# One output unit per hidden tile and whole batch, with the activation computed by Softplus and Erf over four units

## The chip, the core and the metric

The kernel runs on one core of a Trainium2 chip. The metric is the device time of one launch in microseconds (us); lower is better. The core's engines are PE (TensorE: matrix products), DVE (VectorE) and ACT (ScalarE) for elementwise work, POOL (GpSimd) and SP (SyncE), which here mainly issue DMAs. PE multiplies a *stationary* operand, loaded by a weight-load instruction (PEld in the profile), with a *moving* operand that streams through column by column; results go to PSUM, eight banks of 512 fp32 columns, and ACT or DVE copy them out.

## What is computed

```python
def _attn_ref(q, k, v, p):                 # 8 batches, 8 heads, 576 positions, 64 wide; p has 32 packed queries
    p_packed = sm_attn(p, k, v)            # softmax(p k^T / 8) v
    return sm_attn(q, p_packed, p_packed)  # softmax(q p_packed^T / 8) p_packed

def _moe_ref(x, w_in, w_out):              # x: 4608 tokens x 512; w_in 512 x 2048; w_out 2048 x 512
    h = x @ w_in
    sp = np.maximum(h, 0.0) + np.log1p(np.exp(-np.abs(h)))
    g = h * erf(sp)
    return g @ w_out
```

The weights arrive as 64-bit floats and are converted to 32 bits on the chip; everything else is fp32.

## The kernel before

**Tiling.** A batch has 576 tokens, taken as two halves of 288 columns (`HT`). The 2048 hidden features are 16 tiles `f` of 128; a unit is (batch b, half c, pair i of f tiles), 128 units in all. Batches 0 and 1 are gone through in two turns (`TURNS`: first half of the features for both, then the second), so that the weights can arrive meanwhile; batches 2 to 7 each run through all features.

**Products.** Attention's last product is folded into the hidden layer: `w_prime` (L243) multiplies the packed values `pt[b]` with a block of 512 columns of w_in, so that h = a2 x w', with `a2[b]` the second softmax. Precise products are made from values split into a high and a low part of type fp32r (fp32, rounded so that one pass suffices): hi x hi, hi x lo and lo x hi, three matmuls summed in PSUM. In `h_block` (L264) the two f tiles of a unit take 6 matmuls of 288 columns each (two halves r of the contraction, three terms), with w' stationary. In `o_block` (L308) w_out is stationary and g moves: 4 output tiles d x 2 f tiles x 3 terms = 24 matmuls of 288 columns, so the output is built transposed (`outT`) in four PSUM banks, `ps_o0` to `ps_o3`. The first 12 units (`WHOLE`) use unsplit fp32 operands instead, one call per product, because w_out is split later (`split_w_out`, L103, L104).

**The activation** is composed of tables that share a set: ACT halves h on the way out of PSUM (L267, bank pair `ps_h`), then Tanh, Square, Tanh (L270 to L272), DVE two scalar_tensor_tensor (L273, L274), ACT a last Tanh (L275), DVE a product (L283) and the split into `gh` (L286) and `gl` (L287). All of these work on one unit, 576 columns.

**Attention** is a generator of twelve stages: first scores (L165), softmax, transposes (L186), packed values (L198), second scores (L212), transposes and softmax by DVE, split (L232, L233). It and `w_prime` share one PSUM tile of two banks, `ps_m`. It is emitted in stages between the units of the batch before.

**Weights.** `load_f32` loads 64-bit values through SP's queue and converts them by one ACT operation (L87) and three DVE operations (L88 to L90), 512 columns at a time.

**Order.** A plan places loads, attention stages and w' blocks at unit numbers; `o_block` follows `h_block` by `LAG` = 3 units. Within that, a planner orders the instructions of each engine by a simulated timeline (`schedule_with_timeline_sim=True`), the order of emission being the priority. All loads and the first store of a tile go through SP's queue; the second turn of batches 0 and 1 adds onto its output through POOL's queue (L318).

Of the kernel before, what the change touches and what calls it, by code (L numbers as in the profile page):

```python
# [8 lines left out]
F32 = mybir.dt.float32  # L9
# [8 lines left out]

T_SCALE, T_BIAS = 0.2627170245906788, -0.9287499984171923
Q_SCALE, Q_BIAS = 1.2484601345862187, 1.2510285994602417  # L20
U_SCALE, U_BIAS = 2.981034033350855, 0.5025259929887246
A1, A2 = -1.0780370417831138, 7.315330971479113
A_SCALE, A_BIAS = 0.5000167827005251, 0.3105391086974029

# [4 lines left out]
def tile_pack_attention_moe(ctx: ExitStack, tc: tile.TileContext, qT, kT, v, pT, w_in, w_out, outT):  # L29
    nc = tc.nc  # L30
# [5 lines left out]
    NDM = DM // P  # L36
    FB = 512
    NFB = DFF // FB
    NBLK = DFF // (2 * P)
# [5 lines left out]
    LAG = 3  # L45
    NB0 = 2
    TURNS = (0, NBLK // 2, NBLK)
    WHOLE = 12
    SPLIT = 14
    WI_AT = (-1, 1)  # L50
    ATT1 = (0, 2)
    ATT2 = 14
    CONV = 2

    EARLY = ("wpl", "wpl", "wph", "wph", "wpl", "wpl")
# [3 lines left out]
    opool = ctx.enter_context(tc.tile_pool(name="wo", bufs=2 * (DFF // P) + 1))  # L59
    spool = ctx.enter_context(tc.tile_pool(name="stage", bufs=2))  # L60
    wpool = ctx.enter_context(tc.tile_pool(name="wp", bufs=NFB))
    tpool = ctx.enter_context(tc.tile_pool(name="tmp", bufs=3))
# [3 lines left out]

    ident = cpool.tile([P, P], F32, name="ident")
    bias = cpool.tile([P, 4], F32, name="bias")
    w_in_sb = cpool.tile([P, 4, DFF], F32, name="w_in_sb")
    wo, wo_hi, wo_lo = {}, {}, {}  # L70
    nc.scalar.preload_act_table_set("exp_and_others")
    make_identity(nc, ident)
    for i, c in enumerate((T_BIAS, Q_BIAS, U_BIAS, A_BIAS)):
        nc.vector.memset(bias[:, i:i + 1], c)

    def load_f32(dst, src, name, pool=None, tag="wst"):
# [5 lines left out]
        st = (pool or spool).tile([P, n], I64, name=name, tag=tag)  # L82
        nc.sync.dma_start(st[:], src)
        words = st[:].bitcast(U32).rearrange("p (n two) -> p n two", two=2)
        low, high = words[:, :, 0], words[:, :, 1]
        bits = dst.bitcast(U32)
        nc.scalar.activation(dst, high.bitcast(F32), AF.Abs, scale=F64_SCALE)  # L87
# [4 lines left out]
    def load_w_in(j, c, **slot):  # L92
        load_f32(w_in_sb[:, c, j * FB:(j + 1) * FB], w_in[c * P:(c + 1) * P, j * FB:(j + 1) * FB], f"wi{j}_{c}", **slot)

    def load_w_out(f, **slot):
        made = opool.tile([P, DM], F32, name=f"wo{f}", tag="wo")
        load_f32(made[:], w_out[f * P:(f + 1) * P, :], f"wos{f}", **slot)
        wo[f] = made

    def split_w_out(f):  # L100
        hi = opool.tile([P, DM], F32R, name=f"woh{f}", tag="wo")
        lo = opool.tile([P, DM], F32R, name=f"wol{f}", tag="wo")
        nc.scalar.copy(hi[:], wo[f][:])  # L103
        nc.vector.tensor_tensor(lo[:], wo[f][:], hi[:], op=ALU.subtract)  # L104
        wo_hi[f], wo_lo[f] = hi, lo

    a2 = {}
    pt = {}
    wp = {}

    STAGES = 12
    PACKS = 8

    def attention(b, roomy=False):
# [5 lines left out]
        def chunk(name, tag="kvq"):  # L120
            if tag == "kvq":
                return apool.tile([P, S], F32, name=f"{name}_{b}", tag="kvq", bufs=6)[:]
            return tpool.tile([P, S], F32, name=f"{name}_{b}", tag=tag)[:]

        def bank(name):

            turn[0] += 1
            if roomy and turn[0] % 3:
                d = turn[0] % 3 * 2 - 2
                return [ps_o.tile([P, 512], F32, name=f"{name}_{b}_{x}", tag=f"ps_o{d + x}")[:] for x in range(2)], None  # L130
            ps = ps_m.tile([P, 2, 512], F32, name=f"{name}_{b}", tag="ps_m")
            return [ps[:, 0, :], ps[:, 1, :]], ps
# [10 lines left out]
        p = apool.tile([P, NC, NK], F32, name=f"p{b}", tag="p")  # L143
        nc.sync.dma_start(p[:], pT[b])
        k = [chunk(f"k{c}") for c in range(NC)]
        for c in range(NC):
            nc.sync.dma_start(k[c], kT[b, :, c, :])
        yield
        v_at = ("hs", "hs", "hs", "kvq", "kvq") if roomy else ("kvq",) * NCH
        values = [chunk(f"v{j}", v_at[j]) for j in range(NCH)]  # L150
        for j in range(NCH):
            n = min(P, S - j * P)
            nc.sync.dma_start(values[j][0:n, 0:2 * NC * 64], v[b, j * P:j * P + n, :])
        yield
        q_at = ("t0", "t0", "t0", "t1") if roomy else ("kvq",) * NC
        q = [chunk(f"q{c}", q_at[c]) for c in range(NC)]
        for c in range(NC):
            nc.sync.dma_start(q[c], qT[b, :, c, :])
        yield
# [28 lines left out]
        yield  # L188
        banks = bank("p")
# [4 lines left out]
        for j in range(NCH):  # L194
            n = min(P, S - j * P)
            for c in range(NC):
                for r in range(2):
                    nc.tensor.matmul(po[64 * r:64 * r + 64, NK * c:NK * c + NK],  # L198
                                     values[j][0:n, 64 * (2 * c + r):64 * (2 * c + r) + 64],
# [37 lines left out]
    def w_prime(b, j):  # L237
# [8 lines left out]
        nc.vector.tensor_tensor(lo[:], ps[:], hi[:], op=ALU.subtract)  # L246
        wp[b, j] = (hi, lo)

    gs = {}

    def h_block(b, c, i, whole):

# [41 lines left out]
    def o_block(b, c, i, first, last):  # L294
# [16 lines left out]
        if not last:  # L311
            return
# [160 lines left out]
```

## Time and profile before

| | |
|---|---|
| three runs | 790.92, 792.65 (median), 794.25 us |
| profiled execution | 789.89 us; its span from first to last instruction 788.1 us |
| mean granted TensorE clock | 0.968 |
| HBM read, written | 45.61 MB, 11.80 MB |
| matmuls and weight loads | 6256 each |

The profile shows one execution. Busy times of one engine can overlap with those of another, and matmuls of PE overlap with each other: the recorded duration of a matmul contains the way through the array, so the distance between two starts says what one costs in a stream. A group's row reads: line, engine, operation, output<-inputs, shapes, count | busy us, mean ns of one | idle time of the engine just before them, and what ended it. In the slices a digit is a tenth of the slice.

### The profile page before, as it was taken

The page shows a single profiled execution, that of the slowest core. Times are in us where ns is not written, and L with a number is a line of the kernel's source. Part 1 is how long each engine was busy: PE and PEld are TensorE (multiplying, and loading weights), DVE is VectorE, ACT ScalarE, POOL GpSimd, SP SyncE. Part 2 cuts the span into 40 slices and gives each one's busy share as a digit, 9 for nine tenths or more (in the row PEclk, how much of TensorE's full clock was granted, in tenths as well). Part 3 has the DMA queues.
Part 4 walks back from the last instruction along what each step waited for, and adds up shares of the span by engine and source line. Part 5 has one row for each costly group of instructions (what it writes and reads, how often), then busy time and mean ns, then how long its engine had stood idle before and what let it go on. Part 6 is the DMA issues. An engine that isn't in the chain of part 4 may idle for free.

```text
span 788.1 us, 15219 instructions
## 1 busy us (share of the span) xinstructions
PE 744.6 (94%) x6256; PEld 664.1 (84%) x6256; DVE 599.7 (76%) x916; ACT 597.6 (76%) x1011; POOL 15.1 (2%) x22
## 2 busy tenths in 40 slices
PE   3549988999999999999999999999999999999998
PEld 2228756899998898899799998889888998899998
DVE  3887898977689678867887769767886769766664
ACT  3357778988689878887687868778687867878784
POOL 0000000000111100000000000000000000000000
PEclk8568999999999999999999999999999999999999
DMA  8834735002542422013200222002300210000000
GB/s 306 291 110 149 243 116 162 31 17 67 107 88 31 83 76 89 1 39 98 80 32 1 83 81 72 13 1 80 132 32 1 79 47 1 31 2 31 1 31 31
DMA packets 31813, 58.39 MB, mean 74 GB/s; under 512 B 3584, under 2 KB 14848, under 8 KB 31744
## 3 DMA queue, kind: packets, MB, share of 16 engines
q1 hardware_dynamic: 29440, 55.06, 21.5%
q0 software_dynamic: 2304, 2.36, 2.6%
q8 instruction: 49, 0.80, 0.4%
q14 instruction: 20, 0.16, 0.1%
HBM read 45.61 MB, written 11.80 MB: 73 GB/s over the span
## 4 chain that ended last, share of the span: by engine, by line
PE 82%; DVE 7%; DMA 6%; ACT 3%; issue 1%; SPq 0%; ACTq 0%
PE o L308 50%; PE h L264 24%; PE wp L243 4%; DMA wi<-w_in 4%; DMA wos<-w_out 2%; PE p L198 2%; PE s L212 1%; PE s L165 1%; PE t L186 1%; DVE w_in_sb L89 1%; ACT t L270 1%; DVE wo L89 1%; ACT wo L87 1%; DVE w_in_sb L90 1%; DVE g L280 0%
## 5 line engine op out<-in xcount | busy, mean ns | idle before, releaser
L308 PE MATMUL o<-gl,woh 128*128 128x288 f32 x928 | 273.3, 295 | 0.0
L308 PE MATMUL o<-gh,woh 128*128 128x288 f32 x928 | 273.1, 300 | 0.0
L308 PE MATMUL o<-gh,wol 128*128 128x288 f32 x928 | 272.9, 295 | 0.0
L308 PEld LDWEIGHTS o<-gh,woh 128*128 128x128 f32 x928 | 172.1, 187 | 25.5 <-DVE t L273 8.9
L308 PEld LDWEIGHTS o<-gl,woh 128*128 128x128 f32 x928 | 174.3, 188 | 1.8 <-issue 1.3
L308 PEld LDWEIGHTS o<-gh,wol 128*128 128x128 f32 x928 | 174.6, 188 | 1.5 <-issue 1.3
L267 ACT ACTIVATE hs<-h 128x288 f32<-128x288 f32 x256 | 103.2, 412 | 95.4 <-PE h L264 94.6
L264 PE MATMUL h<-a2h,wph 128*128 128x288 f32 x512 | 155.2, 304 | 10.6 <-ACT wph L245 5.9
L264 PE MATMUL h<-a2l,wph 128*128 128x288 f32 x512 | 152.7, 298 | 1.8 <-DVE a2l L233 1.8
L264 PE MATMUL h<-a2h,wpl 128*128 128x288 f32 x512 | 152.6, 298 | 0.0
L283 DVE SCALAR_TENSOR_TENSOR hs<-t,hs 128x576 f32<-128x576 f32 x116 | 87.7, 756 | 72.5 <-ACT t L275 72.5
L275 ACT ACTIVATE t<-t,bias 128x576 f32<-128x576 f32 x128 | 98.8, 772 | 25.3 <-DVE t L274 25.0
L264 PEld LDWEIGHTS h<-a2h,wph 128*128 128x128 f32 x512 | 97.2, 190 | 22.3 <-ACT wph L245 6.8
L273 DVE SCALAR_TENSOR_TENSOR t<-t,hs 128x576 f32<-128x576 f32 x128 | 95.9, 750 | 20.1 <-ACT u L272 19.8
L270 ACT ACTIVATE t<-hs,bias 128x576 f32<-128x576 f32 x128 | 99.6, 778 | 2.9
L271 ACT ACTIVATE t<-t,bias 128x576 f32<-128x576 f32 x128 | 99.3, 775 | 2.3
L264 PEld LDWEIGHTS h<-a2l,wph 128*128 128x128 f32 x512 | 97.4, 190 | 4.3 <-DVE a2l L233 2.8
L272 ACT ACTIVATE u<-t,bias 128x576 f32<-128x576 f32 x128 | 99.3, 776 | 1.8
L264 PEld LDWEIGHTS h<-a2h,wpl 128*128 128x128 f32 x512 | 97.3, 190 | 1.9 <-issue 1.9
L274 DVE SCALAR_TENSOR_TENSOR t<-u,t 128x576 f32<-128x576 f32 x128 | 96.3, 752 | 1.6
L287 DVE TENSOR_TENSOR gl<-hs,gh 128x576 fp32r<-128x576 f32 x116 | 87.3, 753 | 1.5
L286 DVE CAST gh<-hs 128x576 fp32r<-128x576 f32 x116 | 52.9, 456 | 35.0 <-PE o L308 33.8
(60 smaller groups left out, 637.3 us busy)
## 6 DMA issues: line engine op xcount, KB each, us to landing
k<-kT SPq DMA_DIRECT2D x32, 288.0 KB, 4.3
q<-qT SPq DMA_DIRECT2D x32, 288.0 KB, 4.3
outT<-ob SPq DMA_DIRECT2D x64, 144.0 KB, 1.8
wi<-w_in SPq DMA_DIRECT2D x16, 512.0 KB, 6.0
v<-v SPq DMA_DIRECT2D x32, 256.0 KB, 3.6
wos<-w_out SPq DMA_DIRECT2D x16, 512.0 KB, 3.6
outT<-ob POOLq DMA_DIRECT2D x16, 144.0 KB, 3.7
v<-v SPq DMA_DIRECT2D x8, 128.0 KB, 4.2
```

The lines of the kernel that those rows point to most:

```text
L264: nc.tensor.matmul(ps[:, 0:HT], w[:, r, fo:fo + P], a[:, r, c * HT:(c + 1) * HT], start=(n == 0), stop=(n == 5))
L267: nc.scalar.mul(hs[:, k, :], ps[:, 0:HT], 0.5)
L270: nc.scalar.activation(t[:], hs[:], AF.Tanh, bias=bias[:, 0:1], scale=2.0 * T_SCALE)
L271: nc.scalar.activation(t[:], t[:], AF.Square, bias=bias[:, 1:2], scale=Q_SCALE)
L272: nc.scalar.activation(u[:], t[:], AF.Tanh, bias=bias[:, 2:3], scale=U_SCALE)
L273: nc.vector.scalar_tensor_tensor(t[:], t[:], 0.5 * A2, hs[:], op0=ALU.mult, op1=ALU.add)
L274: nc.vector.scalar_tensor_tensor(t[:], u[:], 0.5 * A1, t[:], op0=ALU.mult, op1=ALU.add)
L275: nc.scalar.activation(t[:], t[:], AF.Tanh, bias=bias[:, 3:4], scale=2.0 * A_SCALE)
L283: nc.vector.scalar_tensor_tensor(hs[:], t[:], 1.0, hs[:], op0=ALU.add, op1=ALU.mult)
L286: nc.vector.tensor_copy(ghi[:], hs[:])
L287: nc.vector.tensor_tensor(glo[:], hs[:], ghi[:], op=ALU.subtract)
L308: nc.tensor.matmul(acc[b, c][d][:, 0:HT], w[f][:, d * P:(d + 1) * P], gg[:, k, :], start=(first and k == 0 and n == 0), stop=(last and k = ...
```

## The change

One unit becomes (batch b, one f tile) over the whole 576 columns, still 128 units in the same two turns. What changes in it:

- **Output.** In `o_unit` g is stationary (128 tokens x 128 features) and w_out moves in 512 columns; the output is [token, column] and is no longer transposed. A batch has four full token tiles, one PSUM bank each; its last 64 tokens (`REM`) are copied by a DMA on SP's queue (`keep_rest`, one for each unit) into a tile `rest` beside the 64 of the partner batch, and `Rest` computes the shared 128 rows of two batches in one block of 48 matmuls, in the PSUM tile of attention and w'. Evictions alternate between ACT and DVE.
- **All units are split**: there are no fp32 output products any more, and `load_w_out` splits w_out as soon as it is loaded.
- **Activation.** h is copied out unscaled for four units into one tile of 2304 columns; Softplus and Erf run over it at once; DVE multiplies by h and splits, a unit at a time. The `t` tile has one buffer, `hs` two (of four units), `g` four (of one unit).
- **Lag.** `LAG` is 7 units. The plan has a group's Softplus at the head of the slot after its last h, and Erf and the products a slot later.
- **Weights.** The first 512 columns of w_in come in two halves (`load_w_in(0, 2, c)`, `load_w_in(2, 2, c)`), each with its own w' block, and batch 0's attention is emitted under `tc.high_priority()`.

The diff, cut to its core:

```diff
-    LAG = 3
-    WHOLE = 12
+    G = 4
+    LAG = 2 * G - 1
+    TURNS = (0, NF // 2, NF)
...
+    BUFS = {"hs": 2, "t": 1, "wo": 1, "g": 4, "ob": 2, "kvq": 5}
...
+    def load_w_in(f0, nf, c):
+        cols = slice(f0 * P, (f0 + nf) * P)
+        load_f32(w_in_sb[:, c, cols], w_in[c * P:(c + 1) * P, cols], f"wi{f0}_{c}")
+
+    def load_w_out(f):
...
+        load_f32(whole, w_out[f * P:(f + 1) * P, :], f"wos{f}")
+        nc.scalar.copy(hi[:], whole)
+        nc.vector.tensor_tensor(lo[:], whole, hi[:], op=ALU.subtract)
...
+    def keep_rest(b, f):
+        side = b % 2 * REM
...
+        nc.sync.dma_start(rest_of(f)[:, :, side:side + REM].bitcast(F32), gs[b, f][:, :, NT * P:S].bitcast(F32))
+
+    def h_unit(b, f):
...
+        for c in range(2):
+            ps = ps_h.tile([P, 512], F32, name=f"h{b}_{f}_{c}", tag="h")
...
+            nc.scalar.copy(hs[u // G][:, u % G, c * HT:(c + 1) * HT], ps[:, 0:HT])
-        nc.scalar.activation(t[:], hs[:], AF.Tanh, bias=bias[:, 0:1], scale=2.0 * T_SCALE)
-        nc.scalar.activation(t[:], t[:], AF.Square, bias=bias[:, 1:2], scale=Q_SCALE)
-        nc.scalar.activation(u[:], t[:], AF.Tanh, bias=bias[:, 2:3], scale=U_SCALE)
-        nc.vector.scalar_tensor_tensor(t[:], t[:], 0.5 * A2, hs[:], op0=ALU.mult, op1=ALU.add)
-        nc.vector.scalar_tensor_tensor(t[:], u[:], 0.5 * A1, t[:], op0=ALU.mult, op1=ALU.add)
-        nc.scalar.activation(t[:], t[:], AF.Tanh, bias=bias[:, 3:4], scale=2.0 * A_SCALE)
+    def softplus(k):
+        ts[k] = tmp([P, G, S], F32, f"t{k}", "t")
+        nc.scalar.activation(ts[k][:], hs[k][:], AF.Softplus)
+
+    def gate(k):
+        t, h = ts.pop(k), hs.pop(k)
+        nc.scalar.activation(t[:], t[:], AF.Erf)
+        for i in range(G):
+            b, f = units[k * G + i][:2]
+            nc.vector.tensor_tensor(h[:, i, :], t[:, i, :], h[:, i, :], op=ALU.mult)
+            g = tmp([P, 2, S], F32R, f"g{b}_{f}", "g")
+            nc.vector.tensor_copy(g[:, 0, :], h[:, i, :])
+            nc.vector.tensor_tensor(g[:, 1, :], h[:, i, :], g[:, 0, :], op=ALU.subtract)
+            gs[b, f] = g
+            if b % 2:
+                keep_rest(b, f)
...
+    def evict(po, where, add, on_act):
+        ob = tmp([P, DM], F32, f"ob{where[0][0]}_{len(where)}_{add}", "ob")
+        if on_act:
+            nc.scalar.copy(ob[:], po)
+        else:
+            nc.vector.tensor_copy(ob[:], po)
...
+    def terms(g):
+        return lambda f, cols: ((g[:, 0, cols], wo_hi[f]), (g[:, 1, cols], wo_hi[f]), (g[:, 0, cols], wo_lo[f]))
+
+    def o_unit(b, f, first, last):
+        if b % 2 == 0:
+            keep_rest(b, f)
+        g = gs.pop((b, f))
...
+        for t in range(NT):
+            po = acc[b][t][:]
+            for n, (x, w) in enumerate(terms(g)(f, slice(t * P, t * P + P))):
+                nc.tensor.matmul(po, x, w[:], start=(first and n == 0), stop=(last and n == 2))
+            if last:
+                evict(po, [(b * S + t * P, 0, P)], b in begun, t % 2 == 0)
...
+    class Rest:
+        def run(self, n):
+            for f in range(self.f, min(self.f + n, NF)):
+                for k, (x, w) in enumerate(terms(rest_of(f))(f, slice(0, P))):
+                    nc.tensor.matmul(self.po, x, w[:], start=(f == 0 and k == 0), stop=(f == NF - 1 and k == 2))
...
+        at(k * G + G, "f", ("sp", k))
+        at(k * G + G + 1, "f", ("gate", k))
...
+    def slot(n, o=()):
+        do(n, "f")
+        while late:
+            late.pop(0)()
+        do(n, "pre")
+        if n < N:
+            h_unit(*units[n][:2])
+        do(n, "post")
+        for k in o:
+            o_unit(*units[k])
...
+    for n in range(N + LAG):
+        slot(n, (n - LAG,) if n >= LAG else ())
+        if n < N:
+            b, f, _, last = units[n - LAG]
+            if n >= LAG and last and b % 2 and f == NF - 1:
+                Rest(b, ps_m.tile([P, 2, 512], F32, name=f"rest{b}", tag="m")[:, 0, :]).run(NF)
+            continue
+        tail = tail or Rest(B - 1, ps_m.tile([P, 2, 512], F32, name="rest_tail", tag="m")[:, 0, :])
+        tail.run(2 if n < N + LAG - 1 else NF)
```

The plan for the rest, in words: p and k of a batch are asked for twelve slots into the batch two before it, v and q three and eight slots into the batch before it; attention's nine stages lie between slots 0 and 14 of the batch before; a w' block comes two or three slots ahead of its first unit.

More of the change, by code (lines that the diff above doesn't have):

```diff
@@ L90, in load_f32 @@
         nc.vector.scalar_tensor_tensor(bits, low, 29, bits, op0=ALU.logical_shift_right, op1=ALU.bitwise_or)
[L92 to L104, printed above, removed]
-        wo_hi[f], wo_lo[f] = hi, lo
@@ L141, in copy_out @@
                 nc.scalar.copy(dst[:, x, :], parts[x][:, 0:n])
[L143 to L159, printed above, removed]
+        p, k = loaded.pop(("p", b)), loaded.pop(("k", b))
         a1 = apool.tile([P, 2, S], F32, name=f"a1_{b}", tag="big")
@@ new lines, in slot @@
+    def slot(n, o=()):
[8 more added lines that the diff above has]
+            o_unit(*units[k])
+    with tc.high_priority():
+        load("p", 0)
+        load("k", 0)
+        first = attention(0, roomy=True)
+        next(first)
+        next(first)
+    for c in range(NC):
+        load_w_in(0, 2, c)
+    with tc.high_priority():
+        load("v", 0, "hs")
+        load("q", 0, "t")
+        for _ in range(5):
+            next(first)
+        w_prime(0, 0, 2)
+        next(first)
+        next(first)
@@ L437 @@
+    while late:
+        late.pop(0)()
 def kernel(**inputs):
```

353 lines of the change are left out of this document (144 added, 209 removed).

## The prediction

> **What bounds the kernel now.** I read the page first: busy time by engine, the slices, the chain that ended last.
>
> ```profile
> span 788.1 us, 15219 instructions
> PE 744.6 (94%) x6256; PEld 664.1 (84%) x6256; DVE 599.7 (76%) x916; ACT 597.6 (76%) x1011; POOL 15.1 (2%) x22
> PE   3549988999999999999999999999999999999998
> PEclk8568999999999999999999999999999999999999
> PE 82%; DVE 7%; DMA 6%; ACT 3%; issue 1%; SPq 0%; ACTq 0%
> ```
>
> From the fifth slice or so (about 100 us) PE is full, and 82% of the chain is PE. The profiled execution took 789.89 us, 1.8 us around a span of 788.1; the median of the three runs shown is 792.65. So there are two stages: a start in which PE waits, and a long stage that costs what PE's instructions cost. The chain in order of time gives the long stage's period: the product that makes the packed values (L198) comes once a batch.
>
> ```profile
> 369.21 2.57 PE p L198 x80
> 640.30 2.57 PE p L198 x80
> ```
>
> These are three batches apart: (640.30 - 369.21) / 3 = 90.4 us a batch. The timeline of PE alone says what one instruction costs there: an output matmul, the hidden layer after it, and the fp32 output matmuls of the first units.
>
> ```profile
> 500.04 0.29 PE L308 MATMUL o<-gl,woh 128*128 128x288 f32 x1
> ...
> 502.17 0.29 PE L308 MATMUL o<-gh,wol 128*128 128x288 f32 x1
> 502.30 0.29 PE L264 MATMUL h<-a2h,wph 128*128 128x288 f32 x1
> ...
> 146.84 0.41 PE L308 MATMUL o<-g,wo 128*128 128x288 f32 x1
> 147.81 0.41 PE L308 MATMUL o<-g,wo 128*128 128x288 f32 x1
> ...
> 47.46 0.44 PE L264 MATMUL h<-a2h,wpl 128*128 128x288 f32 x1
> 47.70 0.44 PE L264 MATMUL h<-a2l,wph 128*128 128x288 f32 x1
> ```
>
> The durations overlap, so I go by starts. From 500.04 to 502.17 there are 16 steps: 133 ns for one 288-column matmul. A batch has 192 of L264 and 384 of L308, 576 x 0.1333 = 76.8 us. The other 13.6 us of 90.4 are attention and w'; PE has no idle time left.
>
> **The matmul's step, on which most hangs.** At half clock (47.46 to 47.70; 0.53 granted, windows below) the 288 columns take 240 ns, so at full clock the columns alone are 120, and 133 holds 13 more. The fp32 matmul is issued as two instructions a call (192 for 12 units of 8 calls), and four steps take 0.97 us (146.84 to 147.81; the three starts between are left out): 242 ns each, twice 120 and 2 more. So the 13 is no fixed charge on every matmul. It looks like a floor, the weight load that a 128x288 matmul at full clock is too short to cover. A 512-column matmul streams 120 x 512/288 = 213 and should cover it: I take 213.3 + 2.4 = 215.7 ns. Ends: 213.3, and 237 if time simply goes with columns (133.3 x 512/288); 13.3 as a fixed charge gives 226.7. The value nearest to the 242 ns row, which is nearest in length, is 215.7.
>
> The Trainium skill (TensorE: Matmul & The Clock Gate, section "Wait — 56ns, not 53.3ns?") states columns over 2.4 GHz plus 2.5 ns. It would give 122.5 for 288 columns, where this trace shows 133; the 242 ns row agrees with it. By that rule the new step is 215.8 and the old output loses nothing to loads, which the row refutes.
>
> **The sum on PE.**
>
> ```profile
> L308 PE MATMUL o<-gl,woh 128*128 128x288 f32 x928 | 273.3, 295 | 0.0
> L308 PE MATMUL o<-g,wo 128*128 128x288 f32 x192 | 51.5, 423 | 1.8 <-DVE g L280 1.8
> L243 PE MATMUL wp<-w_in_sb,pt 64*32 64x512 f32 x512 | 41.4, 615 | 8.1 <-DVE ta L215 3.9 <-DVE wpl L246 2.3 <-DVE w_in_sb L90 1.9
> ```
>
> Output before: 3 x 928 x 0.1333 + 192 x 0.2425 = 417.7 us. After: 128 units of 4 token tiles and 3 terms are 1536 matmuls, and the left-over 64 rows of two batches share a tile, 4 pairs x 16 f x 3 = 192; 1728 x 0.2157 = 372.7. Columns are equal if the fp32 ones are counted as three terms (3072 x 288 = 1728 x 512): the gain is purely the floor and the early fp32 units. Hidden layer: 1536 of 288 columns in both, unchanged; w' 33 blocks for 32; attention unchanged.
> In each of the last six batches: 384 x 0.1333 = 51.2 against (192 + 24) x 0.2157 = 46.6. **6 x 4.6 = 27.6 us less**, if PE stays the limit.
>
> **Does PE stay the limit?** The groups by line:
>
> ```profile
> L267 ACT ACTIVATE hs<-h 128x288 f32<-128x288 f32 x256 | 103.2, 412 | 95.4 <-PE h L264 94.6
> L270 ACT ACTIVATE t<-hs,bias 128x576 f32<-128x576 f32 x128 | 99.6, 778 | 2.9
> L222 ACT ACTIVATE ta<-ta 128x1152 f32<-128x1152 f32 x8 | 9.3, 1166 | 9.0 <-DVE ta L221 8.9
> L103 ACT CAST woh<-wo 128x512 fp32r<-128x512 f32 x16 | 10.1, 634 | 0.6 <-DVE wo L90 0.4
> L245 ACT CAST wph<-wp 128x1024 fp32r<-128x1024 f32 x32 | 31.9, 998 | 2.4 <-PE wp L243 2.4
> L138 ACT COPY a1t<-t 128x1024 f32<-128x1024 f32 x8 | 8.1, 1014 | 6.0 <-PE t L186 6.0
> L71 ACT ACT_TABLE_LOAD x1 | 1.3, 1283 | 0.7 <-PEq L465 0.7
> L273 DVE SCALAR_TENSOR_TENSOR t<-t,hs 128x576 f32<-128x576 f32 x128 | 95.9, 750 | 20.1 <-ACT u L272 19.8
> L286 DVE CAST gh<-hs 128x576 fp32r<-128x576 f32 x116 | 52.9, 456 | 35.0 <-PE o L308 33.8
> L287 DVE TENSOR_TENSOR gl<-hs,gh 128x576 fp32r<-128x576 f32 x116 | 87.3, 753 | 1.5
> ```
>
> ACT before, a unit: 2 x 0.41 + 4 x 0.78 = 3.9 us. After, four units: 8 x 0.41, and Softplus and Erf over 2304 columns. Their cost is not in the trace; from L103 to L222 ACT adds 0.532 us for 640 columns, 0.83 ns each, so 1.166 + 1152 x 0.00083 = 2.12 us each (below, nothing: the copies stay; above, four of 576 at 0.78, 3.1 us). Whether they share a table with Exp no row shows: one load serves Tanh, Square and Exp now. Ends: no load, and two loads a group and two more a batch, 10 x 1.28. I take the latter. A batch then has 32 x 0.41 + 8 x 2.12 + 10 x 1.28 = 43, and 12 for attention, w' and evictions: 55 of 86 us, against some 77 of 90 before (16 x 3.9 and 14). DVE: three scalar_tensor_tensor, a cast and a subtract (3.5 us a unit) become a multiply, a cast and a subtract, 1.96. Over the last six batches both lie beside PE and what they lose costs nothing.
> The new evictions of 512 columns (40 and 4, for 80 of 288) alternate ACT and DVE; hidden by the 9 matmuls of the other three banks, 1.9 us. The 128 copies of 64 columns into the left-over tile are new DMAs on SP's queue, each waiting for its g; behind them stand k, p, v, q loads, asked for some three slots (15 us) ahead. I cost them at nothing; uncovered, a batch's attention would start late by a landing of 2 to 4 us. A left-over block (48 matmuls, 10.4 us) holds the PSUM pair of attention and w' once in two batches; they have 16 slots, so I cost that at nothing too, and at its 10.4 us four times if attention became late. Because h and o now lie seven units apart, the final gate (two loads, two wide ACTs, DVE: 9 us) runs under three output units and their share of the left-over rows, 12 us. The end is again a copy and a store, about 3 us.
>
> **The start.** The windows, with the long second one from the first h to the end of batch 1, and the first h in the timeline:
>
> ```profile
> core 0: us, PE busy (x) PEld busy (x) DVE busy (x) ACT busy (x) POOL busy (x), PEclk, DMA share, GB/s
> 30.00:40.00 10.00, 3.18 (x32) 0.48 (x32) 8.67 (x13) 5.76 (x8) 0.00 (x0) 0.50 0.75 277
> 40.00:50.00 10.00, 5.65 (x35) 4.39 (x36) 10.00 (x17) 3.56 (x6) 0.00 (x0) 0.53 0.40 109
> 42.50:246.00 203.50, 188.20 (x1415) 157.08 (x1416) 168.59 (x265) 161.43 (x283) 10.49 (x12) 0.95 0.38 107
> ```
>
> ```profile
> 42.53 0.85 PE L264 MATMUL h<-a2h,wph 128*128 128x288 f32 x2 [4.24 <-ACT a2h L232]
> ```
>
> And DVE's share of the start, by line:
>
> ```profile
> L88 DVE TENSOR_SCALAR wo<-wo 128x512 uint32<-128x512 uint32 x16 | 6.7, 416 | 3.2 <-ACT wo L87 3.1
> L90 DVE SCALAR_TENSOR_TENSOR wo<-wos,wo 128x512 uint32<-128x512 uint32 x16 | 10.9, 684 | 0.0
> L104 DVE TENSOR_TENSOR wol<-wo,woh 128x512 fp32r<-128x512 f32 x16 | 11.0, 685 | 0.7 <-ACT woh L103 0.6
> L233 DVE TENSOR_TENSOR a2l<-tb,a2h 128x1152 fp32r<-128x1152 f32 x8 | 10.8, 1353 | 1.2 <-ACT a2h L232 1.2
> L246 DVE TENSOR_TENSOR wpl<-wp,wph 128x1024 fp32r<-128x1024 f32 x32 | 38.9, 1216 | 6.1 <-ACT wph L245 5.0
> ```
>
> Before the first h DVE is full with conversions. The change converts only two f columns (four half chunks) ahead of w' and gives attention the priority, so the first h comes at about 39 us (36 if DVE never delays attention, 42.5 if nothing is won).
> Before, batches 0 and 1 end at 785 (last matmul) - 6 x 90.4 + 9 (the last has no attention beside it) = 252. From 42.5 that is 209.5, of which PE needs 51.2 (h) + 46.6 + 64 (12 fp32 units, 20 of 3.2) + 27.2 (two attentions and w') = 189; 20.5 are stalls and cold clock.
> After, PE needs 51.2 + 432 x 0.2157 + 27.2 = 171.6. DVE needs 14 w_in chunks of 1.8 us (two shift-and-or of 0.68, a shift of 0.42), 16 w_out of 2.47, 32 gates of 1.96, two attentions of 13.5 (seven operations over 1152 columns at 1.35 and some 4 us of small ones), 8 w' of 1.22: 164. That is nearly PE's need, so the start cannot be as dense: DVE was 83% busy in that window (168.59 of 203.5), and 164 / 0.83 = 198. I take 198 us, from 39 to 237: **15 us less than 252**. Bounds: 184 (PE's need and 12 of stalls), 219 (DVE at 75%).
>
> **Sum:** 789.9 - 27.6 - 15 = 747 on the profiled execution's scale; the runs shown lie 2.8 above it: **750 us**, 5% less.
>
> **Rivals.**
> *Pitch.* The 13 ns belong to every fp32r matmul (226.7 ns), or go with columns (237): +19 to +37, 769 to 787. For it: no 512-column fp32r row exists. Against: the 242 ns row.
> *Start.* With 7 units between h and o, and gates of four, DVE and ACT (some 139 us: 64 copies 26, 16 wide ones 34, 20 loads 26, conversions 31, two attentions and w' 22) take turns at blocking PE: DVE at 75%, 219 us, 771. The other way, PE-limited, 184: 736, with an earlier first h 732.
> *ACT blocks the hidden layer: slower.* h has two PSUM banks, emptied by ACT in order. If a group's Softplus and Erf run back to back, ACT is away 2 x (1.28 + 2.12) = 6.8 us, and both halves of the next h are copied at 7.6; PE meanwhile has o and a slot's share of attention (12 x 0.2157 + 13.6 / 16 = 3.4), h (1.6), and o again: 8.4. The margin is 0.8 us. Each microsecond over it costs 32 us in all; from 2.2 us more a pair (42 us in all) the kernel is slower than before. An a1t copy and a w' cast (1.0 us each) caught between come near, in some groups. If a switch costs twice the load's 1.28 us (what goes ahead of a later load, no row shows), a pair has 2.56 more: 750 + 32 x 1.76 = 806. Against: the plan puts a slot between the two, and then each has its own cover.
> The Trainium skill (ScalarE: Activation LUTs, section "What ACT_TABLE_LOAD costs") speaks for this rival: every switch also drains, about 1380 ns, which the one load here, with nothing ahead of it, cannot show; by it the sum would be some 813.
> *It doesn't do what it says:* the planner scatters the wide activations and holds PE back as much as is saved: 790.
>
> **Chances.** Forecast 0.50 (own range 738 to 762); quicker start 0.10; slower start 0.15; pitch 0.10; no gain 0.03; ACT blocks 0.12. The range leaves out ACT's, no gain, and the top of pitch: 730 to 784. A measurement of this kernel tells about 0.5% from no change: faster 0.85, same 0.03, slower 0.12.
>
> **What would show it.** Steps of 216 ns between output matmuls right, 227 or 237 wrong; L198's counterpart every 86 us; first h near 39; table loads 80 in all; PE idle behind "hs" on ACT in mid-kernel would mean ACT blocks. Wrong if the period exceeds 88 us or batch 1 ends after 250.

## The result, and the profile after

The changed kernel takes **841.7 us** (median of four runs, 839.9 to 846.5) where the kernel before takes 791.8 on the same chip: a ratio of 1.064, with a 95% interval of 1.060 to 1.067. It was forecast 5% faster and is 6% slower; the time lies outside the range. The page of the changed kernel, with its span, busy times, the slices of PE, the chain, and the groups that the forecast had priced:

```profile
span 841.0 us, 12325 instructions
...
PE 754.3 (90%) x5024; PEld 589.4 (70%) x5024; DVE 439.9 (52%) x713; ACT 452.1 (54%) x589; POOL 7.9 (1%) x14
...
PE   3468687989999999989999999899999999899987
...
PE 56%; ACT 21%; DVE 14%; issue 4%; DMA 4%; SPq 0%; DVEq 0%; ACTq 0%
...
L278 DVE TENSOR_TENSOR hs<-t,hs 128x576 f32<-128x576 f32 x128 | 88.5, 754 | 222.3 <-ACT t L275 222.3
...
L270 ACT ACTIVATE t<-hs 128x2304 f32<-128x2304 f32 x32 | 68.1, 2130 | 0.4
...
L270 ACT ACT_TABLE_LOAD x32 | 41.1, 1283 | 0.6
L275 ACT ACT_TABLE_LOAD x32 | 41.1, 1283 | 0.6
```

ACT and DVE have *less* to do than before (452 us against 598, 440 against 600), as forecast, and their prices were right: 2.13 us for a wide operation (2.12 forecast), 0.75 for the multiply, 1.28 for a table load. Yet PE's share of the chain fell from 82% to 56%, and ACT's rose from 3% to 21%. No engine is full any more, which means that they wait for each other. The view of waits of PE's matmuls (who waited for what; us in total, times, longest) says where PE waits:

```profile
PE h L263 <- ACT hs L266: 20.3, 14, 3.2
PE o L314 <- DVE g L280: 13.3, 9, 5.8
...
PE o L314 <- DVE g L281: 3.5, 6, 1.9
```

The hidden layer waits for ACT's copy out of PSUM. This is the rival called "ACT blocks the hidden layer", which had a chance of 0.12 and 806 us. The output matmuls wait nearly as long, 16.8 us, for g, which DVE makes from Erf's result.

How much PE loses, and where, is read from two windows, the first 200 us and the 575 after them: length, PE busy (x matmuls), granted clock, DMA share, GB/s. First the kernel before, then the changed one:

```profile
0.00:200.00 200.00, 159.61 (x1162) 0.87 0.46 148
200.00:775.00 575.00, 575.00 (x5022) 1.00 0.18 49
```

```profile
0.00:200.00 200.00, 145.25 (x1060) 0.82 0.48 155
200.00:775.00 575.00, 551.14 (x3690) 0.99 0.21 58
```

Before, PE idled 40.4 us in the start and never after it. Now it idles 54.8 us in the start and 23.9 us in the stretch after it, and the clock is lower in both. So the loss has two places, and a third thing is in the matmuls themselves. The timeline of PE, one output unit in mid-kernel:

```profile
503.51 0.39 PE L314 MATMUL o<-woh,g 128*128 128x512 f32 x1
...
507.38 0.39 PE L314 MATMUL o<-woh,g 128*128 128x512 f32 x1
```

There are 17 steps between the two rows, 227.6 ns each: not the forecast 215.7 but one of the bounds, 226.7. The product that makes the packed values (L186, once a batch) gives the period:

```profile
305.99 2.23 PE L186 MATMUL p<-a1t,v 128*64 128x32 f32 x66
...
684.82 2.40 PE L186 MATMUL p<-a1t,v 128*64 128x32 f32 x71
```

Four batches in 378.8 us are 94.7 a batch, against 90.4 before and 86 forecast.

### The profile page after: what moved, and what is told of

Read it like the earlier page. It is cut to its first block, busy times and chain, and to the rows that moved or that the text cites. A ratio compares the mean times of both kernels' runs of the same rounds, so it can differ in the third digit from the quotient of the medians.

```text
span 841.0 us, 12325 instructions
## 1 busy us (share of the span) xinstructions
PE 754.3 (90%) x5024; PEld 589.4 (70%) x5024; DVE 439.9 (52%) x713; ACT 452.1 (54%) x589; POOL 7.9 (1%) x14
## 4 chain that ended last, share of the span: by engine, by line
PE 56%; ACT 21%; DVE 14%; issue 4%; DMA 4%; SPq 0%; DVEq 0%; ACTq 0%
PE o L314 26%; PE h L263 18%; ACT t L275 5%; ACT t L270 5%; PE rest L330 4%; DVE hs L278 4%; ACT L270 3%; PE wp L233 3%; ACT L275 2%; DMA stage<-w_in 2%; PE p L186 2%; DVE g L281 2%; DVE g L280 1%; PE s L152 1%; ACT hs L266 1%
## 5 line engine op out<-in xcount | busy, mean ns | idle before, releaser
L314 PE MATMUL o<-woh,g 128*128 128x512 f32 x1024 | 336.0, 401 | 17.5 <-DVE g L280 13.3
L314 PEld LDWEIGHTS o<-woh,g 128*128 128x128 f32 x1024 | 191.8, 191 | 79.6 <-issue 18.7
L266 ACT COPY hs<-h 128x288 f32<-128x288 f32 x256 | 98.5, 399 | 198.3 <-PE h L263 198.3
L278 DVE TENSOR_TENSOR hs<-t,hs 128x576 f32<-128x576 f32 x128 | 88.5, 754 | 222.3 <-ACT t L275 222.3
L314 PE MATMUL o<-wol,g 128*128 128x512 f32 x512 | 201.9, 395 | 0.0
L263 PE MATMUL h<-a2h,wph 128*128 128x288 f32 x512 | 162.5, 319 | 24.5 <-ACT hs L266 20.3
L314 PEld LDWEIGHTS o<-wol,g 128*128 128x128 f32 x512 | 97.1, 190 | 20.4 <-issue 2.6
L281 DVE TENSOR_TENSOR g<-hs,g 128x576 fp32r<-128x576 f32 x128 | 91.2, 751 | 0.6
L270 ACT ACTIVATE t<-hs 128x2304 f32<-128x2304 f32 x32 | 68.1, 2130 | 0.4
L275 ACT ACTIVATE t<-t 128x2304 f32<-128x2304 f32 x32 | 68.1, 2129 | 0.4
L233 PE MATMUL wp<-w_in_sb,pt 64*32 64x512 f32 (+1 forms) x528 | 49.7, 606 | 12.5 <-DVE ta L204 6.6
L280 DVE CAST g<-hs 128x576 fp32r<-128x576 f32 x128 | 53.1, 452 | 3.2 <-PE o L314 3.2
L270 ACT ACT_TABLE_LOAD x32 | 41.1, 1283 | 0.6
L275 ACT ACT_TABLE_LOAD x32 | 41.1, 1283 | 0.6
```

The source lines that it names most:

```text
L233: nc.tensor.matmul(ps[NK * c:NK * c + NK, r, 0:n], pt[b][64 * r:64 * r + 64, NK * c:NK * c + NK], w_in_sb[64 * r:64 * r + 64, c, f0 * P:f0 ...
L263: nc.tensor.matmul(ps[:, 0:HT], w[:, r, fo:fo + P], a[:, r, c * HT:(c + 1) * HT], start=(n == 0), stop=(n == 5))
L266: nc.scalar.copy(hs[u // G][:, u % G, c * HT:(c + 1) * HT], ps[:, 0:HT])
L270: nc.scalar.activation(ts[k][:], hs[k][:], AF.Softplus)
L275: nc.scalar.activation(t[:], t[:], AF.Erf)
L278: nc.vector.tensor_tensor(h[:, i, :], t[:, i, :], h[:, i, :], op=ALU.mult)
```

## The experiments

### The price of a 512-column matmul

Theory: the 13 ns above the columns' own time are a floor under short matmuls, set by the weight load. Rival: they are a charge on every fp32r matmul. This kernel computes nothing of the reference; it runs streams of 36 to 52 matmuls with a new stationary operand each, by type and number of columns.

```diff
+    def stream(kind, n, count, bank):
+        for k in range(count):
+            nc.tensor.matmul(banks[bank][:, 0:n], made[kind][:, k % 3, 128 * (k % 4):128 * (k % 4) + 128],
+                             made[kind][:, 3, 0:n], start=(k == 0), stop=(k == count - 1))
+    stream("r", 288, 39, 3)      # r: fp32r, b: bf16, f: fp32
+    stream("r", 512, 43, 2)
+    stream("b", 288, 44, 3)
+    stream("b", 512, 45, 4)
```

> Computes no output: streams of 36 to 52 matmuls with 128x128 stationary tiles, 128 to 512 columns, in fp32r, bf16 and fp32, accumulating in one bank or alternating between two. The time of it says nothing; the distance of starts does. Floor theory (the prediction's): fp32r steps are 133 ns up to 288 columns and columns x 0.417 + 2.4 ns from some 320 on, 216 at 512. Fixed charge theory: columns x 0.417 + 13 to 14 ns at every width from 256 on, 227 at 512. If bf16 of 512 columns shows 216 in the same run, the charge belongs to fp32r.

The timeline of its PE; the first number of a row is a start, and a row can hold two or three matmuls:

```profile
29.73 0.56 PE L33 MATMUL bank<-src_r 128*128 128x288 f32 x3
...
33.82 0.43 PE L33 MATMUL bank<-src_r 128*128 128x288 f32 x2
...
55.73 0.63 PE L33 MATMUL bank<-src_r 128*128 128x512 f32 x2
...
70.51 0.61 PE L33 MATMUL bank<-src_r 128*128 128x512 f32 x2
71.84 0.41 PE L33 MATMUL bank<-src_b 128*128 128x288 bf16 x2
...
74.78 0.41 PE L33 MATMUL bank<-src_b 128*128 128x288 bf16 x2
...
77.66 0.59 PE L33 MATMUL bank<-src_b 128*128 128x512 bf16 x2
...
83.71 0.59 PE L33 MATMUL bank<-src_b 128*128 128x512 bf16 x2
```

From start to start: fp32r with 288 columns 4.09 us / 31 = 131.9 ns, with 512 columns 14.78 / 65 = 227.4. In bf16, with the same weight loads: 2.94 / 24 = 122.5 and 6.05 / 28 = 216.1. Taken at 0.417 ns a column (120 ns for 288, half of the 240 at half clock), bf16 pays 2.5 ns on top at either length and fp32r 12 to 14. So the charge goes with fp32r, and the floor theory falls. The fp32r streams of 128 and 192 columns cost 110 and 112 ns a matmul: a floor exists, but below 256 columns.

Worked into the forecast: 1728 matmuls x 11.9 ns = **20.6 us** (2.6 a batch).

### Undoing the gate alone

The old activation (Tanh, Square, Tanh, Tanh; no table loads) one unit at a time, with a lag of 3 and buffers to match, everything else as changed.

```diff
-    G = 4
-    LAG = 2 * G - 1
+    G = 1
+    LAG = 3
...
-        nc.scalar.activation(ts[k][:], hs[k][:], AF.Softplus)
-        nc.scalar.activation(t[:], t[:], AF.Erf)
+        nc.scalar.activation(t[:], h[:], AF.Tanh, bias=bias[:, 0:1], scale=2.0 * T_SCALE)
+        nc.scalar.activation(t[:], t[:], AF.Square, bias=bias[:, 1:2], scale=Q_SCALE)
+        nc.scalar.activation(u[:], t[:], AF.Tanh, bias=bias[:, 2:3], scale=U_SCALE)
+        nc.vector.scalar_tensor_tensor(t[:], t[:], 0.5 * A2, h[:], op0=ALU.mult, op1=ALU.add)
+        nc.vector.scalar_tensor_tensor(t[:], u[:], 0.5 * A1, t[:], op0=ALU.mult, op1=ALU.add)
+        nc.scalar.activation(t[:], t[:], AF.Tanh, bias=bias[:, 3:4], scale=2.0 * A_SCALE)
```

> The new tiling with the old activation: Tanh, Square, Tanh, Tanh and three products on DVE for each unit of 576 columns (no table switch, no operation on ACT or DVE longer than some 1.4 us), lag of 3 units. Theory G (Softplus and Erf over four units hold up ACT's other work, and g comes late): period 88.4 to 90 us a batch, PE without visible waits in mid-kernel, some 780 to 800 us. Theory T (the new tiling itself makes PE wait, whatever the activation): period 94 us or more, above 830 us.

803.2 us, ratio 1.014 [1.011, 1.016]. The new gate, with its groups and its lag, costs 38 of the 50 us; the new tiling with the old gate is still slower than the kernel before.

### What in the gate: Erf out of the way, then the loads

The timeline of ACT in the changed kernel, at one group:

```profile
510.65 1.28 ACT L270 ACT_TABLE_LOAD   x1
511.94 2.13 ACT L270 ACTIVATE t<-hs 128x2304 f32<-128x2304 f32 x1
514.09 1.28 ACT L275 ACT_TABLE_LOAD   x1
515.39 2.13 ACT L275 ACTIVATE t<-t 128x2304 f32<-128x2304 f32 x1
517.42 0.68 ACT L266 COPY hs<-h 128x288 f32<-128x288 f32 x2
```

The planner, free to reorder, left nothing between Softplus and Erf. That holds for 22 of the 32 groups (Erf starts 1.3 us after Softplus ends, which is its load); in the other ten, one to three other operations stand between. From 510.65 to 517.42 ACT copies nothing out: 6.8 us, as long as the rival had worked out. What was overrated is the cover. PE at another group, where ACT copied one half of h between the two wide operations:

```profile
565.77 0.30 PE L263 MATMUL h<-a2h,wpl 128*128 128x288 f32 x1
568.50 0.40 PE L263 MATMUL h<-a2h,wph 128*128 128x288 f32 x1 [2.44 <-ACT hs L266]
...
570.59 0.45 PE L263 MATMUL h<-a2h,wpl 128*128 128x288 f32 x1
570.83 0.45 PE L263 MATMUL h<-a2h,wph 128*128 128x288 f32 x1
```

The working had a whole output unit (2.6 us) and a share of attention between two h. Here PE's order has the next half of h right behind the last one, no output matmul between them, and PE stands for 2.44 us. The last two rows show a second price: 2 us after that wait the steps of 288 columns are 240 ns, and they stay so for ten matmuls. PE runs at half clock: the granted clock from 570.6 to 573.9 us is 0.50.

First experiment: by a dependency that orders only, Erf comes no sooner than the second and last copy of the following h unit.

```diff
-        nc.scalar.activation(t[:], t[:], AF.Erf)
+        erf = nc.scalar.activation(t[:], t[:], AF.Erf)
+        if k * G + G < N:
+            after(erf, out_of[k * G + G])       # the copy-out of unit 4k + 4
```

> Erf of a group issues behind the copy-out of the next unit's h, so that Softplus and Erf are not back to back. If ACT's absence of 6.9 us holds up h: PE's waits for hs (50 us at PE and its weight loads) fall by half, 815 to 830 us. If not: within 8 us of 842.

819.1 us, ratio 1.035 [1.033, 1.037], 22 us less than the changed kernel. The second window shows PE idle 13.8 us, for 23.9:

```profile
200.00:775.00 575.00, 561.19 (x3752) 0.99 0.21 57
```

But PE's wait for the copy-out hardly changed in the view of waits (20.3 us without the edit). What is gone is the wait for g, of which 0.5 us is left of 16.8:

```profile
PE h L267 <- ACT hs L270: 19.3, 11, 2.7
...
PE o L320 <- DVE g L287: 0.5, 1, 0.5
```

So spacing the two helps, though not where it was meant to, and is not the whole cure. Why g comes in time in this order was not taken further. Second experiment: take the loads away and keep the wide operations. Tanh shares a table set with Exp, so with Tanh in both places nothing is switched (the output is then another function's).

```diff
-        nc.scalar.activation(ts[k][:], hs[k][:], AF.Softplus)
+        nc.scalar.activation(ts[k][:], hs[k][:], AF.Tanh)
...
-        nc.scalar.activation(t[:], t[:], AF.Erf)
+        nc.scalar.activation(t[:], t[:], AF.Tanh)
```

> The changed kernel with Softplus and Erf both replaced by Tanh, which shares a table set with Exp (output is another function's): the two wide operations of 2.13 us a group stay, the 64 table loads of 1.28 us beside them go, so ACT's absence shrinks from 6.9 to about 4.3 us. If the table loads are what makes the absence longer than the cover (forecast: the margin was 0.8 us), the waits of h for the copy-out go and the six last batches lose most of the 32 us: 800 to 812. If waiting for whole groups of four (g late, two hs tiles) costs by itself, it stays above 825.

**791.0 us**, ratio 0.998 [0.997, 1.000]: 50.7 us less than the changed kernel, and better than the range given for it. PE's and DVE's instructions stand in the same order in both programs, and ACT's differ by the 77 loads alone (64 of the gate, 13 where attention's Exp needs its set back), so nothing else is compared. Its page, waits and windows:

```profile
PE 735.9 (93%) x5024; PEld 580.4 (73%) x5024; DVE 440.9 (56%) x713; ACT 356.0 (45%) x512; POOL 7.8 (1%) x14
...
PE 78%; DVE 9%; ACT 7%; DMA 4%; issue 1%; SPq 0%; DVEq 0%; ACTq 0%
```

```profile
PE h L263 <- ACT hs L266: 6.1, 6, 1.8
...
PE o L314 <- DVE g L281: 3.5, 3, 2.8
PE o L314 <- DVE g L280: 3.4, 2, 3.1
```

```profile
0.00:200.00 200.00, 153.90 (x1153) 0.85 0.49 159
200.00:775.00 575.00, 572.04 (x3830) 1.00 0.21 58
```

PE's idle time from 200 to 775 us goes from 23.9 to 3.0, in the start from 54.8 to 46.1. Over the whole span PE idled 841.0 - 754.3 = 86.7 us in the changed kernel and 790.7 - 735.9 = 54.8 here: 31.9 less, of which the wait for the copy-out is 14.2 (20.3 - 6.1) and the wait for g 9.9 (16.8 - 6.9). The same matmuls were busy 754.3 us there and 735.9 here: 18.4 less. The two make the 50.3 us between the spans. The mean granted clock was 0.947 there and 0.961 here, so the lower clock can have cost 841.0 x 0.053 - 790.7 x 0.039 = 13.7 us of the 18.4; the other 4.7 are not placed. So 99 us of table loads (77 x 1.283) on an engine that was half idle cost 51 us: 32 as waits of PE, 24 of them for h and for g, and some 14 through the clock.

The period shows it too, from the same product:

```profile
289.93 2.64 PE L186 MATMUL p<-a1t,v 128*64 128x32 f32 x80
...
647.34 2.64 PE L186 MATMUL p<-a1t,v 128*64 128x32 f32 x80
```

357.4 / 4 = 89.4 a batch. With the measured pitch PE needs 90.4 - (384 x 0.1333 - 216 x 0.2276) = 88.4. Without loads, mid-kernel is nearly as dense as forecast, and the new tiling is worth 1 us a batch there as measured (90.4 - 89.4) and 2 by what PE needs, not 4.6.

### Smaller and other groups

Softplus and Erf over two units at a time (lag 5), so that a wide operation takes half as long but twice as many loads run:

```diff
-    G = 4
-    LAG = 2 * G - 1
+    G = 2
+    LAG = 5
```

> Softplus and Erf over two units, the same bytes in twice the buffers, lag 5. ACT's absence per pair falls from 6.9 to 4.9 us, with 64 more table loads (82 us of ACT). Theory G: period below 92 us, the time 815 to 830 us. If ACT's total time were the limit, not its long absences: slower than 842 us.

820.4 us, ratio 1.036 [1.033, 1.039]. More loads on ACT and less time: ACT's sum is not what counts. That the shorter absence gained it was expected but is not shown: the lag and the buffers changed with it, and PE's wait for the copy-out is 19.3 us in all, for 20.3. And the old gate over two units, with no loads at all, lands at the same place:

```diff
-    G = 1
-    LAG = 3
+    G = 2
+    LAG = 5
```

> The new tiling with the old activation (no table loads) over two units at once, lag 5; alone over one unit 803. If an operation's fixed cost on ACT and DVE and the short lag of 3 are what is left there: 790 to 797. If four operations of 1.15 us and the two more DVE products block the copy-out as the loads did: 803 to 812.

820.1 us, ratio 1.035 [1.033, 1.037], 17 us more than over one unit. So groups can cost as much without any load. It is hardly the copy-out: PE waits 6.9 us for it here and 5.3 over one unit. Fewer buffers (one for `u`) are an untested reason, and why this order came out worse was not taken further.

### DVE's order within a group

The planner runs four multiplies, then four casts, then four subtracts, so the first g is late. Here each unit is finished before the next begins:

```diff
+            m = nc.vector.tensor_tensor(h[:, i, :], t[:, i, :], h[:, i, :], op=ALU.mult)
+            if i:
+                after(m, split)                 # the previous unit's subtract
```

> DVE must finish a unit's multiply, cast and subtract before the next unit's multiply (the planner had put four multiplies first, then the casts, then the subtracts). If the late first g is what PE waits for: PE's waits on g (30 us at PE and its weight loads) go, 815 to 830 us. If ACT's absence decides: within 8 us of 842.

842.8 us, ratio 1.064 [1.062, 1.067]: no change. The edit did not do away with the wait for g, which is still 13.3 us for the cast:

```profile
PE o L320 <- DVE g L286: 13.3, 5, 7.1
```

So DVE's order within a group is not what makes g late, and this run does not say what that wait is worth.

### The order as it was emitted

Is it the planner's order? All instructions of PE, ACT and DVE were chained in the order of emission, with a group's products spread over three slots; the second kernel also moves the left-over copies.

```diff
+    def chain(*engines):                        # each instruction behind the one emitted before it on its engine
...
+    chain(mybir.EngineType.PE, mybir.EngineType.Activation, mybir.EngineType.DVE)
```

> Edit: PE, ACT and DVE each issue in the order of emission instead of the planner's, and the products of a group of four are emitted over three slots (units 0 and 1, then 2, then 3), so that Softplus, Erf and a unit's multiply, cast and subtract are spread. Theory O: the period falls from 95 to 88.4 us a batch (192 x 0.133 + 216 x 0.228 + 13.6), 6 x 6.4 = 38 us less, some 804 us unless the start suffers. Theory Q: the period stays at 95 us, and the time near 842 us.

> Both edits. If the two losses are separate they add up: Q and O both right 785 to 795 us, O alone some 804, Q alone some 825.

968.2 and 966.7 us (ratios 1.225 [1.220, 1.231] and 1.223 [1.218, 1.229]). A miss: the emitted order is far worse than the planner's everywhere, so these two say nothing of the one place that they were meant for.

### The start

The left-over copies stand in SP's queue and wait there for their g, with weight loads behind them. SP's and ACT's rows in the changed kernel:

```profile
88.59 0.62 SPq L116 DMA_DIRECT2D v<-v  x1
100.29 4.44 SPq L249 DMA_DIRECT2D rest<-g  x4
104.83 0.55 SPq L77 DMA_DIRECT2D stage<-w_in  x1
```

```profile
109.49 0.66 ACT L81 ACTIVATE w_in_sb<-stage 128x512 f32<-128x512 f32 x1 [12.20 <-DMA stage<-w_in]
```

For 11 us nothing is issued, and ACT waits 12.2 us for the chunk behind. Moved to POOL's queue:

```diff
-        nc.sync.dma_start(rest_of(f)[:, :, side:side + REM].bitcast(F32), ...)
+        nc.gpsimd.dma_start(rest_of(f)[:, :, side:side + REM].bitcast(F32), ...)
```

> Edit: the copies of 64 columns into the left-over tile are issued on POOL's queue, not SP's. Theory Q (on SP's queue they wait for g ahead of the weight loads behind them, as at 88.6 to 104.8 us of the changed kernel): batch 1 ends 10 to 20 us earlier, some 825 us in all, the later period of 95 us a batch unchanged. Theory O (the order of ACT's and DVE's work holds PE up): within 5 us of 842.

837.6 us, ratio 1.058 [1.055, 1.062]: 4 us, hardly more than the noise (the two intervals overlap). The wait is there, and worth little. With Erf spaced as above it adds nothing that can be told:

> Erf behind the next h copy-out (alone 819) and the left-over copies on POOL's queue (alone 4 us). If the two causes are separate, 814 to 816; if both only mend the same late start, about 819; below 810 if ACT's wait for the weights was the larger part of what is left.

819.0 us, ratio 1.032 [1.027, 1.036], its runs from 813 to 821. With the old gate of single units:

> The new tiling with the old activation a unit at a time (alone 803) and the left-over copies on POOL's queue. If SP's queue still blocks loads at the start: 796 to 800, level with the kernel before within 1%. If DVE's conversions and splits bound the start: 802 to 804.

805.0 us, ratio 1.016 [1.014, 1.018], nothing gained. Then the same without DVE's part of the conversions:

```diff
-        nc.vector.tensor_scalar(bits, bits, 3, None, op0=ALU.logical_shift_left)
-        nc.vector.scalar_tensor_tensor(bits, high, 0x80000000, bits, op0=ALU.bitwise_and, op1=ALU.bitwise_or)
-        nc.vector.scalar_tensor_tensor(bits, low, 29, bits, op0=ALU.logical_shift_right, op1=ALU.bitwise_or)
```

> The previous run without the three DVE operations that turn a 64-bit weight into 32 bits (ACT's operation stays, so the weights are wrong): some 57 us of DVE work less, all of it before batch 2. If DVE bounds the start, 15 to 25 us less than the previous run; if loads or ACT bound it, within 5 us of it.

801.5 us, ratio 1.011 [1.009, 1.013]: DVE is busy 578.7 us for 624.5, 45.8 less, and 3.5 us are gained. DVE does not bound the start of this kernel, against the forecast's reckoning.

The first h came at 49.7 us (39 was forecast), with DVE full (busy 10.00 of the 10 us from 30 to 40) of conversions and the steps of batch 0's attention. So, on the kernel with one table set, every conversion that the first two f columns don't need was held behind batch 0's last split:

```diff
+        shift = nc.vector.tensor_scalar(bits, bits, 3, None, op0=ALU.logical_shift_left)
+        if 0 in split_of:
+            after(shift, split_of[0])           # batch 0's a2 split on DVE
```

> The kernel with both wide functions as Tanh (alone 791.0, first h at 49.6 us), and on DVE every weight conversion that batch 0's first two f columns don't need held behind batch 0's last split. If these conversions make the first h late: first h at 40 to 43, and if the rest of the start hangs on it, batch 1 ends 6 to 9 us sooner than 266.6 and the time is 782 to 785. If the conversions are then only late in their turn: first h early, time within 3 us of 791 or above it.

The first h in the timeline of PE, in the changed kernel and in this one:

```profile
49.71 0.85 PE L263 MATMUL h<-a2h,wph 128*128 128x288 f32 x2
```

```profile
39.75 0.85 PE L271 MATMUL h<-a2h,wph 128*128 128x288 f32 x2 [8.78 <-ACT a2h L229]
```

The conversions were the delay: the first h comes 10 us sooner, at 39.75. But the time is 793.5 us, ratio 1.002 [1.000, 1.003], 2.4 more than without it. A sooner first h bought this way does not shorten the start; that what was put off is then late in its turn would fit, but is not shown. The same with the old gate over two units, and with the real functions, spaced, and copies on POOL's queue, is worse too:

> The previous run with the conversions held behind batch 0's attention: 6 to 9 us less than it if the first h carries the start, and then below 790, faster than the kernel before; the same or more if the conversions are late in their turn.

> The changed kernel with Softplus and Erf, Erf behind the next h copy-out, left-over copies on POOL's queue (together 819) and the conversions held behind batch 0's attention: 810 to 813 if the first h carries the start, 819 or more if not.

827.9 us, 1.046 [1.044, 1.048] (820.1 without), and 823.2 us, 1.040 [1.037, 1.042] (819.0 without).

Last, what the tiling is worth with one table set and the two remaining suspects mended: copies on POOL's queue, then also groups of two with lag 5.

> Both wide functions as Tanh (alone 791.0) and the left-over copies on POOL's queue (alone 4 us on the changed kernel). If SP's queue holds the start: ACT's 27.6 us of waiting for staged weights mostly go, batch 1 ends 5 to 10 us sooner than 266.6, and the time is 782 to 787, faster than the kernel before by 0.6 to 1.2%. If not: 789 to 792.

> The previous run with groups of two (lag 5, hs four tiles and t two, each of two units), so the first output unit can come two units sooner. If the lag of seven units holds the start: 5 to 8 us less than the previous run; if ACT's fixed costs (64 more operations) or the order weigh more: the same or up to 10 us more.

788.7 us, ratio 0.996 [0.994, 0.998], and **784.4 us, ratio 0.991 [0.988, 0.993]**. The windows of the second:

```profile
0.00:200.00 200.00, 158.90 (x1193) 0.88 0.48 159
200.00:775.00 575.00, 574.14 (x3833) 1.00 0.20 59
```

PE idles 41.1 us in the start, as in the kernel before (40.4). SP's queue is worth 2.3 us here (the intervals overlap) and groups of two with their shorter lag 4.4. So with no table switched, and with less work on ACT and DVE than before, the new tiling comes out 0.9% ahead; with the old activation it is 1.4% behind. With the activation that the reference asks for, no kernel here beats the one before; the nearest is the old gate of single units, 803.2 us.

## Why the prediction was wrong

The difference to be explained is 841.7 - 750 = 91.7 us.

**The price of the output matmul** (step "The matmul's step, on which most hangs"): wrong, 20.6 us. Both observations were right, that an fp32 instruction pays only 2 ns and that an fp32r one pays 13. The inference was not: that a charge absent from another type must be a floor. The 242 ns row differs from the new matmul in *type* as well as in length, and the stream shows that the type decides. The bound 226.7, "a fixed charge", held within a nanosecond, but it had only a rival's chance, 0.10 together with 237. The Trainium skill (TensorE: Matmul & The Clock Gate, section "Wait — 56ns, not 53.3ns?") gives columns over 2.4 GHz plus about 2.5 ns; the bf16 streams agree (122.5 and 216.1), the fp32r ones do not (131.9 and 227.4).

**"Does PE stay the limit?"**: wrong, 50.7 us, the largest step. The working answered with sums: 55 us of ACT in a batch of 86, whose loss "costs nothing". Those sums were near enough, and off the point: PE waits when one result of ACT comes late, however idle ACT is on average. Without the 77 loads, with the same instructions in the same order otherwise, PE's waits fall by 31.9 us. The rival "ACT blocks the hidden layer" had a part of this, the wait for the copy-out (14.2 us), with the absence right (6.8 us). The wait for g (9.9 us) it did not have, and that its 56 us over the forecast are near the 51 measured is luck: it assumed that a switch costs twice 1.28 us. What went against it, "the plan puts a slot between the two", failed: the plan is only an order of emission, and the planner put Erf straight behind Softplus in 22 of 32 groups. Spacing the two gave 22 of the 51 us back. The cover of 8.4 us was counted as if output units stood evenly between the h, and in the row at 568.50 none stands there.

The drain that the Trainium skill (ScalarE: Activation LUTs, section "What ACT_TABLE_LOAD costs") adds to every switch, some 1380 ns, isn't seen here: the load at 514.09 starts 0.02 us after the operation ahead of it ends (511.94 + 2.13). The load's own 1283 ns agree. So that the 63 us of that rule (813 - 750) lie near the 51 measured is luck too.

**The start**: wrong, most of the remaining 20.4 us (791.0 - 750 - 20.6, from the kernel without loads). Some 3 of these are the end, and some 6 are mid-kernel (six batches at 89.4 us for a need of 88.4), both by the profiled executions. The end of batch 1 is reckoned as the forecast did it, from the last matmul back over six periods and 9 us forward. The last matmul of the changed kernel, then of the one without loads:

```profile
834.84 0.39 PE L330 MATMUL rest_tail<-wol,rest 128*128 128x512 f32 x1
```

```profile
784.58 0.39 PE L330 MATMUL rest_tail<-wol,rest 128*128 128x512 f32 x1
```

That gives 276 us (834.8 - 6 x 94.7 + 9), far beyond the 250 that was named as the mark, and 257 without loads, where 237 was forecast (242 with the measured pitch). The forecast carried DVE's share of 83% over as the pace of the start. But DVE was not the pace: with the old activation, 45.8 us less of its work hardly move the start. Nor did a first h 10 us sooner, bought by putting conversions off, gain anything. What the runs do place: at most 2 to 4 us for SP's queue (costed at nothing) and 4.4 us for groups of four with their lag of seven units, beside the loads' own share of the start. The rest is not settled: DVE's conversions, their place before the first h and SP's queue were each tried, and none carries it.

**The end**: 2.7 us more than before (5.8 from the end of the last matmul, 835.2, to the end of the span, against 3.1). The last copy waits for a buffer, `ob` having two, until a store is through, 1.1 us of it after that matmul:

```profile
836.34 0.59 ACT L292 COPY ob_False<-rest_tail 128x512 f32<-128x512 f32 x1 [2.49 <-DMA out<-ob_False]
```

**What held:** the work of ACT and DVE, each duration, the number of table loads (77 and the first; 80 forecast), the left-over block at no price of its own in mid-kernel, and, within 1 us a batch, the density of PE there once the loads are gone (89.4 us against a need of 88.4).

## What to carry to other kernels

Where an engine both empties PSUM for PE and runs long operations, compare its longest absence with what PE has left to do in the *scheduled* order, not its sum of busy time with the period, and do the same for the operand that comes out of those long operations; a table load is part of both. A price for a shape that the trace lacks should come from a row of the same type, even if its length is further off, because the type can carry the charge. An order of emission is not an order of execution when a planner arranges the engines: what a plan "puts between" is to be read from the trace or be bounded as if it weren't there.

## What the runs showed of the hardware

An fp32r matmul of 288 or 512 columns costs 0.417 ns a column and 12 to 14 ns more (131.9 and 227.4 ns), where bf16 pays 2.5; with a new weight load each, none of the fp32r streams went below 110 ns a matmul, the one of 128 columns.

A wait of 2.4 us in a stream that was full before it was followed, 2 us later, by steps at half clock (240 ns for 288 columns). The Trainium skill (TensorE: Matmul & The Clock Gate, section "Part 1: The HAM clock gate (the "warmup" mystery)") puts the drop after at least one idle window of about 3.4 us; here a shorter standstill went ahead of it. In all, the lower clock made some 14 of the 51 us that the table loads cost.
